# The last product of a two-layer network gets its own PSUM bank, and the last output tile leaves in two halves on two queues

## Chip, cores, metric

The kernel runs on one core of one Trainium2 chip. The metric is the device time of one execution in microseconds (us). Times inside an execution come from a profiled run and are counted from the start of its span.

## What is computed

The reference is a delta-rule attention layer followed by a feed-forward block with an exact GELU, all in float32:

```python
# q, k, v: (4 batches, 8 heads, 768 steps, 48); beta: (4, 8, 768)
k_n = k / (norm(k) + 1e-6)
for t in range(S):
    y[t]  = q[t] @ state
    state = state + beta[t] * outer(k_n[t], v[t] - k_n[t] @ state)
x = y as (batch * step, head * dim)        # 3072 x 384
h = x @ w_in                               # w_in: 384 x 2048
out = (0.5 * h * (1 + erf(h / sqrt(2)))) @ w_out   # w_out: 2048 x 384
```

## The kernel before, in words

The 768 steps are cut into NC = 12 chunks of 64 steps. A chunk has two tiles (`tiles[c, a]`, a = 0 and 1), each 128 rows of `x`: 64 steps of two batches. For each chunk the attention part makes `xT`, the transposed input of the feed-forward block. `fc1` (L668) then multiplies it by `w_in` in 16 blocks and puts the GELU of each into `G`. The second matrix product follows from `G` and `w_out_sb`.

For chunks 0 and 1 the second product is done directly (`fc2`, L680). From chunk 2 on it is a Strassen-Winograd scheme over 2 x 2 blocks: seven products of 128 x 1024 by 1024 x 192 instead of eight. `two(c, n)` (L725) issues the matmuls of product n, each product being 16 matmul instructions in the profile, all from L709 in `product`. The order in a chunk is n = 1, 5, 2, 6, 4, 7, 3. The products go to three PSUM tiles: X and Y, each with two halves of 192 columns (`X[:, 0]`, `X[:, 1]`, `Y[:, 0]`, `Y[:, 1]`), and Z. Products 6 and 7 go to `Y[:, 0]` one upon the other, and product 3, the last, goes to `Y[:, 1]`. X and Y come from the pool tag "mlp" (two buffers), which `fc1` uses too; the attention's matmuls use the tag "dn" (two buffers of two banks each).

`read2(c, n)` (L747) combines the products on VectorE after products 6, 7 and 3. After n = 6 it makes `u2` (L751). After n = 7 it makes `u3` (L754), the two halves of tile 1's output (L755, L756), sends tile 1, copies the left half of tile 0's output on ScalarE (L759), and adds Z to `u2` (L760). After n = 3 it makes the right half of tile 0's output (L762) and sends tile 0. Output tiles are 128 x 384 float32; `send` (L675) sends one as two DMAs of 64 rows (96 KB each), both issued from ScalarE's queue.

At the call level a plan gives each step a due time, and `emit` sorts the steps by it. VectorE's instructions stay in that order; the other engines' queues are ordered by the scheduler from the same list. After the last step of the plan only the last chunk's products, reads and sends are left, and then the closing of the program (L992), where the SyncE (SP) queue waits for all DMAs and the engines meet in a barrier. SP's queue otherwise carries the input loads; its last load is issued at 545.2 us.

The last chunk's c is NC - 1 = 11. Nothing but its closing steps is touched by the change.

Of the kernel before, what the change touches and what calls it, by code (L numbers as in the profile page):

```python
# [11 lines left out]
ALU = mybir.AluOpType  # L12
# [4 lines left out]
def kernel(  # L17
# [28 lines left out]
    nc = tc.nc  # L46
    B, H, S, D = q.shape
    DM, DF = moe_w_in.shape
    C = 64
    HB = 32  # L50
    NC = S // C
# [6 lines left out]
    HALF = [slice(0, C), slice(C, 2 * C)]  # L58
# [10 lines left out]
    def dn(name):  # L69
        return ps.tile([128, 2, 512], F32, tag="dn", name=name)  # L70
# [20 lines left out]
    tiles = {}  # L91
# [7 lines left out]
    for c in range(NC):  # L99
        for a in range(NA):  # L100
            u = tiles[c, a] = Unit()
# [61 lines left out]
    for p in range(2):  # L163
        nc.gpsimd.dma_start(out=bt[:, :, p, :],
                            in_=beta.rearrange("b h (c t) -> (b h) c t", t=C))
# [497 lines left out]
    DH = DM // 2  # L663
    B11, B12 = w_out_sb[:, 0:FH, 0:DH], w_out_sb[:, 0:FH, DH:]
    B21, B22 = w_out_sb[:, FH:, 0:DH], w_out_sb[:, FH:, DH:]
# [6 lines left out]
                             rhs=xTs[c][:, m, :], start=(m == 0), stop=(m == NM - 1))  # L672
        nc.scalar.activation(G[:, f, :], psH, ACT.Gelu)  # L673

    def send(u):  # L675
        for p in range(2):
            row = (2 * u.a + p) * S + u.c * C
            nc.scalar.dma_start(out=out[row:row + C, :], in_=u.o[HALF[p]])

    def fc2(u, f0, f1):  # L680
        if f0 == 0:
            u.psO = ps.tile([128, DM], F32, tag="mlp", name="psO")
        for f in range(f0, f1):
            nc.tensor.matmul(u.psO, lhsT=G[:, f, u.a * 128:(u.a + 1) * 128],  # L684
                             rhs=w_out_sb[:, f, :], start=(f == 0), stop=(f == NF - 1))
        if f1 == NF:
            u.o = wk.tile([128, DM], F32, tag="o_sb", name="o_sb")
            nc.scalar.copy(u.o, u.psO)
            send(u)
# [14 lines left out]
    A = [[G[:, k * FH:(k + 1) * FH, a * 128:(a + 1) * 128] for k in range(2)] for a in range(NA)]  # L704
    W2 = {}

    def product(ps_, lhs, rhs, first):
        for f in range(FH):
            nc.tensor.matmul(ps_, lhsT=lhs[:, f, :], rhs=rhs[:, f, :], start=first and f == 0,  # L709
                             stop=f == FH - 1, skip_group_check=not first)  # L710
# [14 lines left out]
    def two(c, n):  # L725
        if n == 1:
            W2["X"] = ps.tile([128, 2, DH], F32, tag="mlp", name="psX2")
            W2["o"] = [wk.tile([128, DM], F32, tag="o_sb", name="o_sb") for a in range(NA)]
            product(W2["X"][:, 0], A[0][0], B11, True)
        elif n == 5:  # L730
            W2["Z"] = small[0].tile([128, DH], F32, tag="z", name="psZ2")
            product(W2["Z"], W2["S"], T[1], True)
            W2["p1"] = more[0].tile([128, DH], F32, tag="p1", name="p1")
            nc.scalar.copy(W2["p1"], W2["X"][:, 0])
        elif n == 6:
            W2["Y"] = ps.tile([128, 2, DH], F32, tag="mlp", name="psY2")
            product(W2["Y"][:, 0], A[0][0], T[2], True)
        elif n == 2:
            product(W2["X"][:, 0], A[0][1], B21, False)
        elif n == 7:  # L740
            product(W2["Y"][:, 0], A[1][0], T[3], False)
        elif n == 4:
            product(W2["X"][:, 1], A[1][1], T[4], True)
        else:
            product(W2["Y"][:, 1], A[0][1], B22, True)

    def read2(c, n):  # L747
        o, X, Y, Z = W2["o"], W2["X"], W2["Y"], W2["Z"]
        if n == 6:
            W2["u2"] = more[0].tile([128, DH], F32, tag="u2", name="u2")  # L750
            nc.vector.tensor_tensor(W2["u2"], Y[:, 0], W2["p1"], op=ALU.add)  # L751
        elif n == 7:
            W2["u3"] = more[0].tile([128, DH], F32, tag="u3", name="u3")
            nc.vector.tensor_tensor(W2["u3"], Y[:, 0], W2["p1"], op=ALU.add)  # L754
            nc.vector.tensor_tensor(o[1][:, 0:DH], X[:, 1], W2["u3"], op=ALU.add)  # L755
            nc.vector.tensor_tensor(o[1][:, DH:], Z, W2["u3"], op=ALU.add)  # L756
            tiles[c, 1].o = o[1]
            send(tiles[c, 1])
            nc.scalar.copy(o[0][:, 0:DH], X[:, 0])  # L759
            nc.vector.tensor_tensor(W2["u2"], Z, W2["u2"], op=ALU.add)  # L760
        else:
            nc.vector.tensor_tensor(o[0][:, DH:], Y[:, 1], W2["u2"], op=ALU.add)  # L762
            tiles[c, 0].o = o[0]
            send(tiles[c, 0])

    def first_layer(c, f):
        fc1(c, f)
# [3 lines left out]
    def second_layer(c, n):  # L771

        two(c, n)
        if n in (1, 2):
            for h in range(2):
                mix(c, n + 1, h)
        elif n in (6, 7, 3):
            read2(c, n)
# [218 lines left out]
```

## Time and profile before

| | us |
|---|---|
| median of 5 runs | 678.8 |
| lowest and highest run | 677.83 and 679.25 |
| the profiled execution, its own time | 677.83 |
| its span, from first to last instruction | 675.8 |
| TensorE busy (share of the span) | 643.7 (95%) |
| VectorE busy | 450.7 (67%) |
| ScalarE busy | 221.0 (33%) |
| the last product's matmuls, start | 668.49 |
| last instruction on a compute engine, end | 671.76 |

The time of an execution is longer than its span by what lies before the first and after the last instruction. In the timeline a row gives start, duration, engine, line, operation, output tile, input tiles and count. In square brackets stands how long the engine was idle before it and what ended that. PE is TensorE's matmuls, PEld its weight loads, DVE VectorE, ACT ScalarE. ACTq and SPq are the queues of ScalarE and SyncE: a DMA_DIRECT2D there is the issue of a DMA, and the transfer itself comes later. A DMA's landing is when its last semaphore update is seen.

### The profile page before, as it was taken

How to read it: one execution, taken by the hardware profiler on the slowest of the kernel's cores; microseconds unless marked ns; L12 is line 12 of the kernel's file. 1: busy time of each engine (PE TensorE's matmuls, PEld its weight loads, DVE VectorE, ACT ScalarE, POOL GpSimd, SP SyncE). 2: the span in 40 equal slices, each digit the busy share in tenths (PEclk: the TensorE clock that was granted, in tenths of full speed). 3: DMA queues.
4: the chain of work that ended last, by engine and by line, in shares of the span. 5: the costliest groups of instructions: out<-in, count | busy, mean ns of one | idle time of the engine just before them, and what ended most of it. 6: DMA issues, size and time to landing. Idle time of an engine off the chain costs nothing.

```text
span 675.8 us, 21674 instructions
## 1 busy us (share of the span) xinstructions
PE 643.7 (95%) x9542; PEld 561.4 (83%) x9542; DVE 450.7 (67%) x920; ACT 221.0 (33%) x571; POOL 90.0 (13%) x91
## 2 busy tenths in 40 slices
PE   6858999998999999999999999999999999999997
PEld 5656875765689989989989989989989989989996
DVE  5999999895589856579846479846479844324021
ACT  3357754213443142242153142153142132132220
POOL 5051300302210021111021111021111010000000
PEclk9975999998999999999999999999999999999999
DMA  8875565203431233421232411211401310100101
GB/s 124 190 239 171 116 172 131 48 1 58 87 42 32 55 43 55 75 41 26 55 46 51 81 34 25 52 23 31 66 3 25 56 18 3 25 1 2 23 1 25
DMA packets 157566, 39.75 MB, mean 59 GB/s; under 512 B 149216, under 2 KB 152288, under 8 KB 157472
## 3 DMA queue, kind: packets, MB, share of 16 engines
q1 hardware_dynamic: 151424, 33.06, 25.7%
q10 hardware_dynamic: 5952, 5.12, 3.4%
q8 instruction: 75, 1.23, 0.8%
q0 software_dynamic: 96, 0.20, 0.1%
q14 instruction: 19, 0.16, 0.1%
HBM read 33.62 MB, written 4.72 MB: 57 GB/s over the span
## 4 chain that ended last, share of the span: by engine, by line
PE 75%; DVE 5%; issue 1%; POOL 0%; ACT 0%
PE psH L671 32%; PE psY L709 12%; PE psX L709 12%; PE psZ L709 4%; PE psJ L511 3%; PE psK L566 3%; PE psG L361 3%; PE psO L684 2%; PE psU L591 2%; DVE tmp L436 2%; PE psY L609 2%; DVE Nu L438 2%; PE psY L618 1%; PE psX L653 1%; DVE u L754 0%
## 5 line engine op out<-in xcount | busy, mean ns | idle before, releaser
L671 PE MATMUL psH<-xT,w_in_sb 128*128 128x256 f32 x1152 | 262.3, 384 | 2.9 <-ACT G L673 2.2
L671 PEld LDWEIGHTS psH<-xT,w_in_sb 128*128 128x128 f32 x1152 | 216.0, 191 | 34.5 <-ACT G L673 3.9
L673 ACT ACTIVATE G<-psH 128x256 f32<-128x256 f32 x192 | 73.4, 384 | 187.1 <-PE psH L671 175.1
L438 DVE TENSOR_TENSOR Nu<-Nu,tmp 128x30 f32<-128x30 f32 (+9 forms) x180 | 61.8, 343 | 6.2
L436 DVE TENSOR_TENSOR tmp<-Nu 128x30 f32<-128x30 f32 (+9 forms) x180 | 62.2, 346 | 5.1
L709 PE MATMUL psY<-w_out_sb,G 128*128 128x192 f32 x320 | 57.0, 329 | 1.1 <-DVE u L754 0.5
L709 PE MATMUL psX<-w_out_sb,G 128*128 128x192 f32 x320 | 56.2, 329 | 0.0
L709 PEld LDWEIGHTS psY<-w_out_sb,G 128*128 128x128 f32 x320 | 51.6, 190 | 2.8 <-DVE u L754 2.5
L709 PEld LDWEIGHTS psX<-w_out_sb,G 128*128 128x128 f32 x320 | 52.2, 190 | 0.7
L684 PE MATMUL psO<-w_out_sb,G 128*128 128x384 f32 x128 | 46.6, 507 | 0.2 <-DVE w_out_sb L237 0.2
L654 ACT COPY xT<-psX 128x384 f32<-128x384 f32 x24 | 11.4, 478 | 106.6 <-PE psX L653 105.5
L303 POOL TENSOR_TENSOR n<-n,half 128x16 f32<-128x16 f32 x10 | 29.5, 2950 | 89.1 <-DVE n L286 68.2
L597 ACT COPY U<-psU 64x192 f32<-64x192 f32 x96 | 30.1, 313 | 19.5 <-PE psU L591 18.3
L396 DVE TENSOR_TENSOR P<-psG,mask 128x1024 f32<-128x1024 f32 x10 | 12.2, 1221 | 35.9 <-PE psG L361 35.9
L684 PEld LDWEIGHTS psO<-w_out_sb,G 128*128 128x128 f32 x128 | 23.5, 194 | 14.1 <-DVE w_out_sb L237 0.8
L326 POOL TENSOR_TENSOR V<-V,n 128x384 f32<-128x384 f32 x22 | 21.8, 1001 | 95.1 <-DMA V<-in_v_dram 94.4
L460 POOL MEMSET Zf<- 32x512 f32 x23 | 12.4, 540 | 153.7 <-DVE Zf L451 125.2
L574 DVE TENSOR_TENSOR W<-psK,V 128x384 f32<-128x384 f32 x22 | 12.1, 552 | 30.6 <-ACT y L573 30.5
L718 DVE TENSOR_TENSOR S<-G 128x512 f32<-128x512 f32 x20 | 13.7, 687 | 25.8 <-ACT G L673 25.7
L632 DVE TENSOR_TENSOR x<-psY,y 64x192 f32<-64x192 f32 x80 | 28.2, 353 | 0.9
L709 PE MATMUL psY<-T,G 128*128 128x192 f32 x160 | 28.2, 329 | 0.0
L709 PE MATMUL psX<-T,G 128*128 128x192 f32 x160 | 28.0, 329 | 0.0
(135 smaller groups left out, 856.3 us busy)
## 6 DMA issues: line engine op xcount, KB each, us to landing
Kp<-in_k_dram SPq DMA_DIRECT2D x76, 96.0 KB, 3.4
w_out_sb<-in_moe_w_in_dram SPq DMA_DIRECT2D x24, 256.0 KB, 3.9
V<-in_v_dram SPq DMA_DIRECT2D x48, 96.0 KB, 2.9
out_dram<-o_sb ACTq DMA_DIRECT2D x48, 96.0 KB, 2.2
w_raw<-in_moe_w_out_dram SPq DMA_DIRECT2D x10, 384.0 KB, 4.0
Zf<-in_moe_w_out_dram SPq DMA_DIRECT2D x6, 384.0 KB, 4.8
Qp<-in_q_dram SPq DMA_DIRECT2D x64, 32.0 KB, 2.2
Qp<-in_q_dram SPq DMA_DIRECT2D x16, 96.0 KB, 4.2
```

The costliest lines, as they stand in the source:

```text
L303: nc.gpsimd.tensor_tensor(flat, flat, half, op=ALU.pow)
L326: engine.tensor_tensor(u.V, u.V, ns[u.c][:, u.a].unsqueeze(2).to_broadcast([128, H, D]), op=ALU.mult)
L361: nc.tensor.matmul(psG[HALF[p], r, i * NP + j, :], lhsT=u.Kt[rows, p, j, :], rhs=(u.Qt if x else u.Kt)[rows, p, j, :], start=True, stop=True)
L436: nc.vector.tensor_tensor(tmp, nu[:, j + 1:, j:j + 1].to_broadcast([128, n, j]), nu[:, j:j + 1, 0:j].to_broadcast([128, n, j]), op=ALU.mult)
L438: nc.vector.tensor_tensor(nu[:, j + 1:, 0:j], nu[:, j + 1:, 0:j], tmp, op=ALU.add)
L511: nc.tensor.matmul(psJ[to, i, :], lhsT=(xm if level else off)[rows, u, :], rhs=zf[rows, u, HB:C] if level else xm[rows, u, :], start=True, ...
L597: copy(pairs(u.U[HALF[p]], s), u.psU[HALF[p ^ s], p])
L632: nc.vector.tensor_tensor(dst, src, pairs(u.y[HALF[p ^ s]], s), op=ALU.add)
L671: nc.tensor.matmul(psH, lhsT=w_in_sb[:, f // 2, m, f % 2 * 128:(f % 2 + 1) * 128], rhs=xTs[c][:, m, :], start=(m == 0), stop=(m == NM - 1))
L673: nc.scalar.activation(G[:, f, :], psH, ACT.Gelu)
L684: nc.tensor.matmul(u.psO, lhsT=G[:, f, u.a * 128:(u.a + 1) * 128], rhs=w_out_sb[:, f, :], start=(f == 0), stop=(f == NF - 1))
L709: nc.tensor.matmul(ps_, lhsT=lhs[:, f, :], rhs=rhs[:, f, :], start=first and f == 0, stop=f == FH - 1, skip_group_check=not first)
```

## The change

For the last chunk alone:

- Product 3 is written to a PSUM tile of its own, `psV2`, from the tag "dn", instead of `Y[:, 1]`. L762 reads it there.
- Tile 0's left half (columns 0 to 191) is sent once it has been copied, by two DMAs of 64 rows from SP's queue.
- Tile 0's right half (columns 192 to 383) is sent after L762 by two DMAs of 64 rows, the upper one from SP's queue and the lower one from ScalarE's.

`send` takes the columns and the queues as arguments. The other chunks and tile 1 send as before. The program has two more DMAs than before.

```diff
-    def send(u):
+    def send(u, cols=slice(0, DM), queues=(nc.scalar, nc.scalar)):
         for p in range(2):
             row = (2 * u.a + p) * S + u.c * C
-            nc.scalar.dma_start(out=out[row:row + C, :], in_=u.o[HALF[p]])
+            queues[p].dma_start(out=out[row:row + C, cols], in_=u.o[HALF[p], cols])
...
         else:
-            product(W2["Y"][:, 1], A[0][1], B22, True)
+            W2["V"] = W2["Y"][:, 1] if c < NC - 1 else dn("psV2")[:, 0, 0:DH]
+            product(W2["V"], A[0][1], B22, True)
...
             nc.scalar.copy(o[0][:, 0:DH], X[:, 0])
             nc.vector.tensor_tensor(W2["u2"], Z, W2["u2"], op=ALU.add)
+            tiles[c, 0].o = o[0]
+            if c == NC - 1:
+                send(tiles[c, 0], slice(0, DH), (nc.sync, nc.sync))
         else:
-            nc.vector.tensor_tensor(o[0][:, DH:], Y[:, 1], W2["u2"], op=ALU.add)
-            tiles[c, 0].o = o[0]
-            send(tiles[c, 0])
+            nc.vector.tensor_tensor(o[0][:, DH:], W2["V"], W2["u2"], op=ALU.add)
+            if c == NC - 1:
+                send(tiles[c, 0], slice(DH, DM), (nc.sync, nc.scalar))
+            else:
+                send(tiles[c, 0])
```

## The prediction

> **What bounds the kernel now.** The page comes first, to see whether a saving at the very end can be hidden by anything.
>
> ```profile
> span 675.8 us, 21674 instructions
> ...
> PE 643.7 (95%) x9542; PEld 561.4 (83%) x9542; DVE 450.7 (67%) x920; ACT 221.0 (33%) x571; POOL 90.0 (13%) x91
> ...
> PE 75%; DVE 5%; issue 1%; POOL 0%; ACT 0%
> ```
>
> TensorE is busy for 95% of the span, and the chain that ended last runs over it. The change leaves TensorE's 9542 matmuls and their shapes as they are, and touches only the last chunk, so I read the timeline of the last microseconds:
>
> ```profile
> start us, us, engine line op out<-in xcount [idle before <-releaser]
> ...
> 665.28 2.76 PE L709 MATMUL psY<-w_out_sb,G 128*128 128x192 f32 x16
> 668.08 0.36 DVE L754 TENSOR_TENSOR u<-psY,p 128x192 f32<-128x192 f32 x1 [4.77 <-PE psY L709]
> 668.47 0.36 DVE L755 TENSOR_TENSOR o_sb<-psX,u 128x192 f32<-128x192 f32 x1
> 668.49 2.57 PEld L709 LDWEIGHTS psY<-w_out_sb,G 128*128 128x128 f32 x16 [0.74 <-DVE u L754]
> 668.49 2.87 PE L709 MATMUL psY<-w_out_sb,G 128*128 128x192 f32 x16 [0.45 <-DVE u L754]
> ...
> 668.90 0.32 ACT L759 COPY o_sb<-psX 128x192 f32<-128x192 f32 x1 [13.51 <-DVE o_sb L755]
> 669.01 0.35 DVE L760 TENSOR_TENSOR u<-psZ,u 128x192 f32<-128x192 f32 x1
> 669.12 3.84 ACTq L678 DMA_DIRECT2D out_dram<-o_sb  x4
> 671.40 0.36 DVE L762 TENSOR_TENSOR o_sb<-psY,u 128x192 f32<-128x192 f32 x1 [2.04 <-PE psY L709]
> ```
>
> Everything ends in one file. The seventh product (n = 7) ends at 668.04. VectorE reads it (L754), and only when that read is over (668.44) does the last product (n = 3) start, at 668.49. L762 follows, then the two DMAs of tile 0. The DMAs are in the view of line L678 over these microseconds:
>
> ```profile
> L678 ACTq DMA_DIRECT2D out_dram<-o_sb x4: 473/542/619, 669.1 to 672.3; - x4
> L678 ACTq EVENT_SEMAPHORE  x2: 17/17/17, 668.9 to 671.8; - x2
> ...
> DMA to landing us min/median/max: 2.1/2.2/2.3
> ```
>
> Durations are in ns (min/median/max). The same timeline in narrow windows puts the last two issues at 671.84 (0.47 us) and 672.34 (0.62 us): ACT's queue hands them over one after the other. The last one lands 2.3 us after its issue, at 674.6. SP's queue has been waiting for exactly this, by the view of its waits:
>
> ```profile
> SPq L992 <- DMA out_dram<-o_sb: 128.9, 2, 128.3
> ```
>
> From 674.6 to 675.8 come SP's remaining closing waits and the barrier of the engines. No compute engine works after 671.76, so whatever makes that last landing earlier shortens the span one for one.
>
> **What the Trainium skill says.** "PSUM — Partial Sum Buffer", section "PSUM bank collisions raise a hardware error", asks that accesses by two engines be ordered by bank and quadrant, not by address. The trace agrees in effect: the product into Y[:,1] waits for a read of Y[:,0]. "DMA: Bandwidth & Descriptors", section "Issuing engines are not separate DMA queues", says that issuing from two engines saves only the sequencer's issue time, since the 16 DMA engines are the same. Here that issue time is on the path. "Perfetto Trace Analysis", section "DMA Instruction — HWDGE (DVE, Sync)", says that two sequencers share one descriptor generator, locked while one uses it. The kernel's start, where SP and ACT both issue at 0.80, shows a mild form: 0.72 and 0.73 us for those two issues, against a median of 0.64 over SP's four.
>
> **The change part by part.** The program as built differs only in these tail instructions; every earlier row on every engine has the same waits.
>
> *Own bank.* For the last chunk the last product goes to psV2, and its first matmul no longer waits for VectorE. The buffer's pool, "dn", was last read by L632, long before, so nothing new is waited for. The three products before it start at 660.08, 662.68 and 665.28, 2.60 apart. So this one starts at 665.28 + 2.60 = 667.88, not 668.49 (0.61 saved), and takes 2.76 as they do, not 2.87 (0.11). It ends at 670.64 in place of 671.36: **0.72 us**, all of it on the path. L754, L755, L756 and L760 keep their times, since they depend on n = 7 (668.04); L760 ends at 669.36, before 670.64. L762 moves whole, to 670.67 to 671.03.
>
> *First half (columns 0 to 191) sent early.* Two DMAs of 48 KB on SP, released by ACT's copy L759, which ends at 669.22. At up to 0.62 each they occupy SP's queue until about 670.6, which is 0.5 us before it is needed again. Ahead of them stand input loads that were issued before 546. Their 96 KB mix with tile 1's 192 KB, which flow from about 670.2 to 671.5 now (141 GB/s over 1.4 us). At that rate 288 KB last to about 672.2, and the final data begin then (below). I cost this at nothing; the cover is the last product and DMA latency. With the cover gone it is 0.3 us at most.
>
> *Second half on two queues.* SP and ACT each send 48 KB after L762. L762's end to the first issue is 0.08 now (671.76 to 671.84), so both issue at 671.11. ACT is free: tile 1's two issues end at 670.25 now. The issue that counted was the second, at 672.34; of the 1.23 us between 672.34 and 671.11, 0.72 is the product and **0.50** is the first issue that no longer stands ahead. From issue to landing: 2.1 for an issue that starts on an empty queue, 2.3 for one behind another, both for 96 KB. Each transfer is now half, but two start together and may contend for the generator. The trace has no such pair of output transfers, so I bound it. Low: 1.8, the fastest of SP's small input transfers late in the kernel (16 and 32 KB). High: 2.3 and another 0.45. That is the delay at the start, where the other queue's data begin at 2.75 against 2.30 although both issued at 0.80; those were 512 pieces each, these are 64. I take 2.2. The landing is then at 671.11 + 2.2 = 673.3, against 674.6: **1.3 us** in all so far, of which 0.72 is the product.
>
> *Closing waits.* After its last wait ends SP goes through further semaphores of its list: five rows between 674.6 and 674.9, some 0.065 us each. In the program of before the last output DMA is on the second pair of the list. With two more DMAs, the last pair is on the third and fourth, so two rows fewer follow: **0.13 us**. From the landing to the end 1.2 becomes 1.05. SP reaches this list only after its own last issue (about 671.7), well before 673.3. The moved assignment of `o` emits nothing.
>
> *Sum.* 0.72 + 0.50 + 0.1 + 0.13 = 1.45 us. The profiled execution took 677.83 (span 675.8 and 2.0 around it), so its like would take 676.4. It was the fastest of the five runs; from the median 678.8 I get **677.4**.
>
> **The rivals.**
>
> 1. *Forecast:* gain 1.1 to 1.75 us (landing 2.55 to 1.9), 677.05 to 677.7.
> 2. *The two issues still go one after the other.* The lock or the shared engines make the later half land 2.75 after its issue. Gain 0.72 + 0.13 + 0.05 = 0.9, time 677.9. For: the 0.45 at the start. Against: there, four issues on each queue took 3.05 us in all, not the sum of both.
> 3. *The product keeps its wait*, or TensorE has another reason to stand (the change doesn't do what it says). Only the split is left, 0.7 us: 678.1. For: a gap is put down to the latest releaser, and another may stand behind it. Against: the operands of n = 3 were there by 660.97 (end of L723).
> 4. *Slower: two queues at once are dear.* At the start, with both queues issuing, landing took 4.0 to 6.2 us, median 5.1. Were the last pair to take 5.1, the end is at 671.11 + 5.1 + 1.05 = 677.3, 1.5 later: 680.3. It turns into a loss from 3.6 us. Against: those transfers were loads in 192-byte pieces with others queued behind; SP's queue is empty here, and the pieces are 768 bytes.
>
> **How the numbers follow.** A difference of 0.2% is 1.36 us, about what a measurement of this kernel can tell from no change, and the forecast lies just beyond it. Rival 1 gets 0.76 (0.62 beyond the bound, 0.14 short of it), rival 2 0.12, rival 3 0.06, rival 4 0.06 (0.05 past the bound, 0.01 short of it). So faster 0.62, same 0.33, slower 0.05. The range takes in rivals 1 to 3 (677.05 to 678.1) and about 0.4 for the median of runs that lie 1.4 us apart: 676.6 to 678.4.
>
> **What the profile after would show.** No idle before the last 16 matmuls, and their start 2.60 after those of n = 7; DVE's last row about 670.7; two issues on SP at about 669.3 and one each on SP and ACT near 671.1; the last landing near 673.3; a span near 674.3. The forecast is wrong if the last product still starts after L754's read, if SP's and ACT's last issues differ by 0.4 or more in length, if they land more than 2.6 us after issue, or if tile 1's transfers run past 672.3 and push the last pair.

## The result, and the profile after

| | before | after |
|---|---|---|
| median, us | 678.69 (47 runs) | 676.18 (26 runs) |
| lowest and highest run | 676.36 and 681.97 | 674.61 and 678.14 |
| the profiled execution, its own time | 677.83 | 674.98 |
| its span | 675.8 | 673.2 |

The ratio is 0.9969, with a 95% interval of 0.9959 to 0.9978: 2.1 us faster, from 1.5 to 2.8. The means of these runs (678.44 and 676.31) differ by 2.1 too, the medians by 2.5. The forecast was 1.45 us and a median of 677.4, within 676.6 to 678.4; the measured median lies below that range. One more run of the change, at 680.24, is on record and not among the 26; the part on the rest of the 2.1 us comes back to it.

The timeline of the last microseconds of after:

```profile
664.20 2.76 PE L709 MATMUL psY<-w_out_sb,G 128*128 128x192 f32 x16
...
666.80 2.76 PE L709 MATMUL psV<-w_out_sb,G 128*128 128x192 f32 x16
667.00 0.36 DVE L755 TENSOR_TENSOR u<-psY,p 128x192 f32<-128x192 f32 x1 [4.77 <-PE psY L709]
...
667.93 0.35 DVE L761 TENSOR_TENSOR u<-psZ,u 128x192 f32<-128x192 f32 x1
668.05 2.44 ACTq L678 DMA_DIRECT2D out_dram<-o_sb  x3
668.17 2.28 SPq L678 DMA_DIRECT2D out_dram<-o_sb  x3
669.60 0.36 DVE L766 TENSOR_TENSOR o_sb<-psV,u 128x192 f32<-128x192 f32 x1 [1.32 <-PE psV L709]
```

The last product now starts 2.60 after n = 7, before VectorE has read Y, and has no idle time ahead of it. DVE's last sum waits 1.32 for it where it waited 2.04. SP's queue appears with three issues.

The view of line L678 from 669.5 on shows the last pair, and the view of SP's waits what SP waited for (the closing, L992 before, is now L998):

```profile
L678 SPq DMA_DIRECT2D out_dram<-o_sb x1: 466/466/466, 670.0 to 670.0; - x1
L678 ACTq DMA_DIRECT2D out_dram<-o_sb x1: 498/498/498, 670.0 to 670.0; - x1
```

```profile
SPq L678 <- ACT o_sb L760: 83.9, 1, 83.9
SPq L998 <- DMA out_dram<-o_sb: 1.5, 2, 1.0
```

Both queues issue at 669.99, and the two issues hardly stretch each other: 0.47 us on SP and 0.50 on ACT (the first of the two on ACT's queue took 0.47 before). SP's 128 us of waiting at the end have become 83.9 for the left half and 1.5 for the landings.

**Where the 2.1 us are.** The two profiles differ by 2.6 us of span, but n = 7 itself starts at 664.20 in place of 665.28. The instruction stream up to there is the same, so 1.08 us are not the change's (where they come from is read further down). From n = 7's start to the end it is 10.49 before and 9.01 after, 1.48 less. I measure this stretch, "the tail", in the trace of every run below: in traces with the same closing it repeats within 0.02 us, where times scatter by over 3 us. A second number repeats too, the time of an execution less its span: its median is 2.05 before (2.00 to 2.13 in the 59 runs beside the first experiments) and 1.78 after (1.72 to 1.90 in 27 runs). So the change gives 1.48 + 0.27 = 1.75 us, and 0.35 of the 2.1 is open. The experiments take these three in turn.

### The profile page after: what moved, and what is told of

Read it like the earlier page. It is cut to its first block, busy times and chain, and to the rows that moved or that the text cites. A ratio compares the mean times of both kernels' runs of the same rounds, so it can differ in the third digit from the quotient of the medians.

```text
span 673.2 us, 21678 instructions
## 1 busy us (share of the span) xinstructions
PE 645.0 (96%) x9542; PEld 562.1 (84%) x9542; DVE 450.9 (67%) x920; ACT 220.9 (33%) x571; POOL 89.6 (13%) x91
## 4 chain that ended last, share of the span: by engine, by line
PE 76%; DVE 4%; issue 0%; POOL 0%; ACT 0%
PE psH L671 32%; PE psX L709 12%; PE psY L709 12%; PE psZ L709 4%; PE psJ L511 3%; PE psK L566 3%; PE psO L684 3%; PE psG L361 3%; PE psU L591 2%; DVE tmp L436 2%; PE psY L609 2%; DVE Nu L438 2%; PE psY L618 1%; PE psX L653 1%; PE psV L709 0%
## 5 line engine op out<-in xcount | busy, mean ns | idle before, releaser
L709 PE MATMUL psY<-w_out_sb,G 128*128 128x192 f32 x304 | 54.1, 329 | 0.6
L709 PEld LDWEIGHTS psY<-w_out_sb,G 128*128 128x128 f32 x304 | 49.1, 190 | 2.1 <-DVE u L755 1.8
L684 PE MATMUL psO<-w_out_sb,G 128*128 128x384 f32 x128 | 48.0, 519 | 0.2 <-DVE w_out_sb L237 0.2
```

## The experiments

A summary first. Counted from the first matmul of n = 7 (us), by the records of each trace:

| kernel | n = 7 at | last product starts | last issue | last landing | end (tail) | time less span (median) |
|---|---|---|---|---|---|---|
| before | 665.28 | 3.21 | 7.07 | 9.32 | 10.49 | 2.05 |
| the change | 664.20 | 2.60 | 5.79 | 7.91 | 9.01 | 1.78 |
| e1_bank | 663.96 | 2.60 | 6.35 | 8.60 | 9.76 | 2.05 |
| e2_split | 666.97 | 3.21 | 6.51 | 8.65 | 9.75 | 1.79 |
| e3_one_queue | 665.98 | 2.60 | 6.30 | 8.29 | 9.33 | 2.04 |
| g2_sp_both | 665.78 | 2.60 | 6.30 | 8.27 | 9.31 | 1.73 |
| e4_whole_rows | 666.47 | 2.60 | 5.84 | 8.27 | 9.43 | 1.77 |
| f3_list_end | 665.39 | 2.60 | 5.79 | 7.93 | 8.90 | 1.75 |
| f4_again | 669.58 | 2.60 | 5.79 | 7.92 | 9.01 | 1.77 |

By these columns the 1.48 us are 1.28 of the last issue (0.72 of the product, 0.51 of the issue that stood ahead, 0.05 between the sum's end and the first issue, which was about 0.08 and is 0.03), 0.13 of the way from issue to landing (2.25 to 2.12) and 0.07 of what follows the landing (1.17 to 1.10).

### The two parts alone

e1_bank keeps the own bank and sends as before:

```diff
-            if c == NC - 1:
-                send(tiles[c, 0], slice(0, DH), (nc.sync, nc.sync))
...
-            if c == NC - 1:
-                send(tiles[c, 0], slice(DH, DM), (nc.sync, nc.scalar))
-            else:
-                send(tiles[c, 0])
+            send(tiles[c, 0])
```

> Only the own bank of the last product; tile 0 is sent whole after L762's sum, both DMAs on ACT's queue, as before. Theory T (the tail's sum is right, and what the measured median gained beyond 1.5 us is not made by the edit): from the first matmul of n = 7 to the end of the span 10.5 us become 9.75 (0.7 less); the time 0.7 us below before, 0.9990. Rival R (the edit also shortens something outside the tail, through the bank): the span from the start to n = 7 is shorter in every run, or the time outside the span falls from 2.0 to 1.8 us here, and the time gains 1.0 us or more, 0.9985 or less.

e2_split keeps the sends and puts the last product back:

```diff
-            W2["V"] = W2["Y"][:, 1] if c < NC - 1 else dn("psV2")[:, 0, 0:DH]
+            W2["V"] = W2["Y"][:, 1]
```

> Only the sends: halves, on the queues of the change; the last product stays in Y[:, 1] and waits for the read of Y[:, 0]. Theory T: from n = 7's start to the end 10.5 becomes 9.7 to 9.8 (0.75 less: 0.5 for the second issue, 0.1 for the landing, 0.13 for the closing waits); time 0.75 us below before, 0.9989. Rival R (the split also shortens the time outside the span, since SP now ends with its own DMAs): the time less the span is 1.8 us in place of 2.0 and the time gains 1.0 us, 0.9985.

The timeline of e2_split has the old gap back:

```profile
670.19 2.87 PE L709 MATMUL psY<-w_out_sb,G 128*128 128x192 f32 x16 [0.45 <-DVE u L755]
```

The bank alone takes 0.73 off the tail, the sends alone 0.74; together 1.47, the whole 1.48. The two parts add up because they lie one behind the other on one path. (psV2 is another tile as well as another bank; which of the two the wait belonged to was not tried.) The times agree but tell less: 0.9993 (0.9982 to 1.0004) for the bank, where 0.73 us is 0.9989, and 0.9987 (0.9971 to 1.0004) for the sends, where 0.74 + 0.26 us is 0.9985. Rival R was right about the sends in its second number: with them the time less span is 1.79, with the bank alone 2.05.

### What the second queue and the halves are worth

e3_one_queue sends both pieces of the right half from ACT:

```diff
-                send(tiles[c, 0], slice(DH, DM), (nc.sync, nc.scalar))
+                send(tiles[c, 0], slice(DH, DM), (nc.scalar, nc.scalar))
```

> The change, but both DMAs of the right half on ACT's queue; the left half still early on SP's. Theory T (the issue that stands ahead is what the second queue takes away): the second issue starts 0.5 us after the first and lands 2.1 after its start; from n = 7's start to the end 9.4 us, 0.45 more than with the change. Rival (the two issues share one generator, so two queues gain nothing): the end within 0.1 of the change's 9.0.

The view of L678 around its last two issues:

```profile
L678 ACTq DMA_DIRECT2D out_dram<-o_sb x2: 473/540/607, 671.8 to 672.3; - x2
...
DMA to landing us min/median/max: 1.9/1.9/2.0
```

For the simultaneous pair of the change the same view in f4_again, where the landings are on record, has:

```profile
DMA to landing us min/median/max: 1.9/2.0/2.1
```

The second issue is 0.51 later than in the change, but the end only 0.32. Issued one behind the other, 48 KB land in 1.86 and 1.99 us, while the later one of the pair takes 2.12: that returns 0.13. Another 0.06 comes back in SP's closing list (9.33 less 8.29 is 1.04, where the change has 1.10; f3_list_end below shows why). The tail lies a little below theory T's 9.4 and well above the rival's 9.1. The times said only 0.9992 (0.9977 to 1.0006).

g2_sp_both sends both pieces from SP (`(nc.sync, nc.sync)`).

> The change with both DMAs of the right half on SP's queue, so that ACT's program has 662 instructions. Theory T for the path: as with e3_one_queue the second issue stands 0.5 us behind the first, 9.33 us from n = 7's start to the end. For the time less the span: 1.78 under both theories of the count; 2.05 would be against both.

9.31: which queue does it alone makes 0.02 us. Its ratio was 0.9974 (0.9947 to 1.0001).

e4_whole_rows keeps the two queues and drops the early left half: in e1_bank's form, the last call is `send(tiles[c, 0], queues=(nc.sync, nc.scalar))` in the last chunk.

> The change without the early left half: tile 0 goes whole (rows of 1536 bytes) after the last sum, upper rows on SP's queue, lower on ACT's. Theory T: twice the bytes in the last pair land 0.3 us later and the closing list is two rows longer (0.13): 9.4 us from n = 7's start to the end. Rival (landing is fixed latency, bytes cost nothing): 9.1 to 9.15, the closing rows alone.

```profile
DMA to landing us min/median/max: 2.2/2.3/2.4
```

That is the last pair's line in its view of L678: 96 KB each land in 2.2 and 2.4 us. The tail is 9.43, as theory T had it, in other parts: the last landing is 0.36 later (8.27 against 7.91, of which 0.03 is the later issue), and what follows it 0.06 longer (1.16 against 1.10), not 0.13. The ratio was 0.9982 (0.9970 to 0.9993).

Four kernels with the own bank make a square: whole rows on one queue have a tail of 9.76 (e1_bank), whole rows on two queues 9.43, halves on one queue 9.33, halves on two 9.01. The halves are worth 0.42 to 0.43 us with either, the second queue 0.32 to 0.33.

f3_list_end moves the last pair to the end of SP's closing list, by four smaller loads of V in the last chunk in place of two:

```diff
-            fetch_in(u.V, v, u)
+            if c == NC - 1 and a == 1:
+                for p in range(2):
+                    for r in range(2):
+                        rows = slice(c * C + r * HB, c * C + (r + 1) * HB)
+                        nc.sync.dma_start(out=u.V[p * C + r * HB:p * C + (r + 1) * HB],
+                                          in_=v[2 * a + p, :, rows, :].rearrange("h t d -> t h d"))
+            else:
+                fetch_in(u.V, v, u)
```

> The change, with the last chunk's second V tile loaded by four DMAs of 32 rows in place of two of 64 (around 508 us, off the path), so that every later DMA takes a semaphore two places on, and the last pair gets those that SP's closing list checks last. If the list's order is on the path as the prediction had it: 8.88 us from n = 7's start to the end, 0.13 less than the change, and the time 0.13 below it (not to be told by the times). If the rows are hidden behind the landing: 9.0.

The tail is 8.90, 0.11 less, with the landing 0.02 later. From the last landing to the end 1.10 becomes 0.97, by two rows: about 0.065 us for each row of the list that is left after the last landing. The rows from the last landing on are these in before and in the change:

```profile
L992 SPq EVENT_SEMAPHORE  x5: 28/28/28, 674.6 to 674.9; - x5
```

```profile
L998 SPq EVENT_SEMAPHORE  x4: 28/28/28, 672.1 to 672.3; - x4
```

So the change itself saved one row, not the two of the prediction. Its last pair stands third and fourth on the list, but ACT's half, which lands last, is the third. f3_list_end is by its tail the fastest version, and by its times (676.25, ratio 0.9965, 0.9950 to 0.9981) not to be told from the change.

### The time outside the span

In the first six kernels 2.05 us went with 665 instructions in ACT's program and 1.78 with 664. (The counts are of the program as built; the traces have 30 more rows on ACT in every kernel, 695 in before.) f1_act_row adds one to the change:

```diff
             nc.scalar.copy(W2["p1"], W2["X"][:, 0])
+            if c == NC - 1:
+                nc.scalar.copy(W2["p1"], W2["X"][:, 0])
```

> The change with one more instruction on ACT's queue: p1 is copied twice in the last chunk (L734), in ACT's 13 us of idle time. In six kernels the time less the span was 2.05 us where ACT's program has 665 instructions (before, e1_bank, e3_one_queue) and 1.77 to 1.79 where it has 664 (the change, e2_split, e4_whole_rows). Theory A (ACT's instruction count decides): 2.05 here, with 665. Theory B (it is that SP issues one of the last DMAs, which the same three do): 1.78 here. From n = 7's start to the end 9.0 us under both.

2.06, tail 9.01. f2_tile1_sp takes one from before, and leaves the closing as it was:

```diff
-            send(tiles[c, 1])
+            send(tiles[c, 1], (nc.sync, nc.scalar) if c == NC - 1 else (nc.scalar, nc.scalar))
```

> Before, with tile 1's upper rows in the last chunk sent from SP's queue: ACT has 664 instructions, and the last two DMAs are still both ACT's. Theory A: the time less the span is 1.78 us. Theory B: 2.05. From n = 7's start to the end 10.5 us under both, since the last product's wait and ACT's two last issues stand.

1.79, tail 10.50. Theory B is out, in both directions: one row on ACT's queue, off the end's path, moves 0.27 us outside the span. The ratios, 0.9977 (0.9965 to 0.9989) and 1.0001 (0.9988 to 1.0015), agree with 1.48 us alone and 0.27 us alone (0.9978 and 0.9996). I then varied the count alone, by small copies early on ACT's queue (n = 2, 8, 3, 9, 17, 33, 65):

```diff
+            for _ in range(n if c == NC - 1 else 0):
+                nc.scalar.copy(lim[:, 1:2], lim[:, 0:1])
```

> The change with two more small copies (128 x 1) on ACT's queue, in idle time early on: ACT's program has 666 instructions. Counts so far: the time less the span is 2.05 us at 665 (four kernels) and 1.78 at 664 (five). If it is odd against even counts: 1.78. If it is a limit between 664 and 665: 2.05. From n = 7's start to the end 9.0.

> The change with eight more small copies on ACT's queue: 672 instructions, a multiple of eight like 664. If even counts, or multiples of eight, are what saves the time: 1.78 us of time less span. If it is a limit between 664 and 665: 2.05. From n = 7's start to the end 9.0.

> The change with three more small copies on ACT's queue: 667 instructions. The limit between 664 and 665 fell: with 666 and 672 the time less the span was 1.82 and 1.70 us. If odd counts cost the 0.28: 2.05 here. If 665 was only a special value: 1.75 to 1.8. From n = 7's start to the end 9.0.

> The change with nine more small copies on ACT's queue: 673 instructions, 8 above 665. If what counts comes back every 8 instructions: time less span 2.05 us. If it comes back every 16 or more, or 665 is single: 1.7 to 1.8. From n = 7's start to the end 9.0.

> Seventeen more small copies: 681 instructions, 16 above 665. Period of 8 or 16: time less span 2.05 us. Period of 32 or more, or single: 1.7 to 1.8.

> Thirty-three more small copies: 697 instructions, 32 above 665. Period of 8, 16 or 32: time less span 2.05 us. Period of 64, or single: 1.7 to 1.8.

> Sixty-five more small copies: 729 instructions, 64 above 665. Any period from 8 to 64: time less span 2.05 us. Single: 1.7 to 1.8. The copies may hold up ACT's work near 120 us, so the span itself may be longer; from n = 7's start to the end 9.0.

| ACT instructions | 662 | 664 | 665 | 666 | 667 | 672 | 673 | 681 | 697 | 729 |
|---|---|---|---|---|---|---|---|---|---|---|
| time less span, us | 1.73 | 1.75 to 1.79 | 2.04 to 2.06 | 1.82 | 1.73 | 1.70 | 1.82 | 1.75 | 1.75 | 1.75 |

All seven have a tail of 9.01 to 9.02. The 1.70 is from three runs. A limit, parity, or a period of 8, 16, 32 or 64 does not explain it: 665 is the only costly count found. The rows of the whole program do not explain it either, since e3_one_queue and g2_sp_both both have 21677 and 2.04 and 1.73 us. That the 0.27 us come and go with ACT's program is shown; why 665 is dear stays open, and a part of the change's gain is therefore an accident of this kernel's count. Five of the seven had ratios of 0.9962 to 0.9982. i_act_33 and i_act_65 were slower as wholes, 1.0005 and 1.0037: their copies stand at 79 to 88 us and 77 to 98 us, between the steps by which ACT prepares the weights (L224), and these two traces lose about 2 and 4 us between 75 and 120 us.

### The rest of the 2.1 us

f4_again is the change once more.

> The change itself once more, beside before on the same chip. Theory T (1.48 us of span and 0.28 around it, the rest of the first 2.1 is where the runs fell): 1.76 us below before, 0.9974, interval reaching over 0.9969. Rival R (something else in the runs is made faster, 0.3 to 0.6 us): 0.9969 or less again, and 0.9974 at the edge of the interval or out of it. In the profile 9.0 us from n = 7's start to the end, whatever n = 7's own start.

Its ratio was 0.9984 (0.9970 to 0.9999), 1.1 us. Theory T's 0.9974 lies inside this interval and rival R's 0.9969 just outside. The two measurements, weighted by the inverse square of their half widths (0.00095 and 0.00145), give 0.9974 (0.9966 to 0.9981), where theory T's 1.75 us is 0.9974.

A stronger test of rival R takes all runs on record. A run's time less its kernel's tail and its time outside the span is what lies ahead of n = 7. That is 665.95 us in the mean of 259 runs of before, and 666.08 in 138 runs of the change (twice) and six of its variants (e1_bank, e2_split, e3_one_queue, g2_sp_both, e4_whole_rows, f1_act_row), with standard errors of 0.08 and 0.11. This takes the tail to be the same in every run of a kernel, as it is in the traces. No gain ahead of n = 7 shows, where rival R needs 0.3 to 0.6 us, so it falls: the 0.35 is where the first runs fell.

Why single measurements swing is seen in the runs of the first one. Nearly all lie in three groups, 1.3 us apart:

| group | before, us | after, us | difference of the group medians |
|---|---|---|---|
| low | 676.36 to 676.88 (8 runs) | 674.61 to 675.08 (7) | 1.65 |
| middle | 677.34 to 678.26 (13) | 675.85 to 676.35 (9) | 1.68 |
| high | 678.64 to 679.67 (24) | 677.13 to 678.14 (10) | 1.62 |

(Two runs of before, 681.69 and 681.97, and the run of the change at 680.24 are a fourth group.) Within a group the difference is 1.6 to 1.7 us. The medians differ by more because before's lies in its high group and after's in its middle one.

The windows of both profiles show where a run falls into its group. The columns are the stretch, its length, busy time and number of instructions on PE, PEld, DVE, ACT and POOL, the granted clock, DMA share and GB/s. Before:

```profile
150.00:153.00 3.00, 2.96 (x19) 1.50 (x13) 3.00 (x3) 0.00 (x0) 0.51 (x1) 1.00 0.02 5
153.00:156.00 3.00, 0.38 (x18) 0.29 (x22) 2.72 (x5) 0.98 (x2) 2.76 (x5) 1.00 0.04 7
156.00:160.00 4.00, 4.00 (x130) 2.47 (x125) 2.50 (x4) 1.15 (x2) 1.71 (x1) 0.57 0.53 99
...
165.00:640.00 475.00, 473.32 (x7144) 425.77 (x7137) 300.29 (x633) 141.98 (x351) 51.68 (x43) 1.00 0.23 39
```

After:

```profile
150.00:153.00 3.00, 3.00 (x31) 2.03 (x28) 3.00 (x3) 0.00 (x0) 0.48 (x1) 0.50 0.02 5
153.00:156.00 3.00, 3.00 (x5) 1.08 (x4) 2.75 (x5) 0.98 (x2) 2.76 (x5) 0.50 0.03 7
156.00:160.00 4.00, 3.98 (x137) 2.45 (x136) 2.17 (x4) 1.15 (x2) 1.74 (x1) 0.97 0.53 99
...
165.00:640.00 475.00, 473.32 (x7135) 426.00 (x7134) 300.11 (x633) 141.36 (x351) 51.07 (x43) 1.00 0.23 39
```

Around 153 to 156 TensorE has few matmuls to run (18 and 5). In before the half clock comes after that pause, at 156 to 160, and slows the 130 matmuls there. In after it comes ahead of the pause and in it, at 149 to 156, and is mostly over when the work comes. From 165 to 640 both are alike to the last digit (473.32). The same matmul, found in both traces by its place in the order, shows what this cost:

| the matmul that starts in before at, us | 149.0 | 152.2 | 156.0 | 160.1 | 165.1 | 640.2 |
|---|---|---|---|---|---|---|
| after starts it later (+) or earlier (-) by, us | +0.04 | +2.50 | +0.27 | -1.08 | -1.08 | -1.08 |

After loses 2.5 us at half clock where before does not, gets most of it back in the pause, and then does not lose what before loses. That is the whole 1.08 us of n = 7's start. All 18 traces agree. From the matmul at 149.0 to the one at 165.1 they take 1.1 to 1.5 us less than before where the half clock falls ahead of the pause or in it, or is missing (ten traces). They take the same within 0.1 us where it follows the pause for 3.4 us (before and four more), and 1.05 to 1.15 more where it lasts for longer after the pause (e4_whole_rows, f2_tile1_sp, f4_again). Six traces, f4_again among them, have another stretch of half clock near 68 to 76 us, and each loses 2.78 us there. These steps are about the distances between the groups: f4_again has both losses, and its own time, 680.35, is in the fourth.

The Trainium skill, "TensorE: Matmul & The Clock Gate", section "What's actually happening", says that the clock gate follows TensorE's activity in windows of 3413 ns that run free of the kernel's start. The traces agree in that their stretches at half clock, but for the last, which the end of the trace cuts off, are 3.4 us or whole multiples of it. That the clock makes the groups is read from 18 traces; no experiment moved the windows.

## Why the prediction was wrong, point by point

- **Own bank, 0.72 us: right.** The last product starts 2.60 after n = 7 and ends at 5.36; e1_bank gave 0.73. Rival 3 is out.
- **Left half early, nothing: right.** Its two SP issues (0.55 and 0.68 us) are over 0.5 us before the last one, and the packets of tile 1 and the left half end at 670.6, before those of the last pair begin at 671.1.
- **Two queues, 0.50 and 0.1 us: right,** with 0.56 and 0.13 measured. The pair's issues hardly stretched each other, so rival 2's lock did not show, and the later landing took 2.12 us where 2.2 was taken. The two terms are not one cause each: the second queue alone is worth 0.32 and the halved bytes 0.42.
- **Closing list, 0.13 us: mis-sized, 0.07.** The prediction counted two rows fewer; it was one, since ACT's half landed last and stands third on the list. f3_list_end shows that two rows are 0.13.
- **The sum for the span: right, in part by luck.** The tail is 9.01, where the working gives 9.05. The list gave 0.06 less than predicted, the last issue 0.06 more, of which 0.05 is the shorter way from the sum to the first issue.
- **"Span 675.8 and 2.0 around it": the first step that failed.** The 2.0 was carried over as a constant. It fell by 0.27 us, and f1_act_row and f2_tile1_sp show that this goes with the one row that ACT's program lost when one of its last issues went to SP. No row of the profile shows this time; only the time beside the span does. Why 665 rows cost it stays open.
- **"About 0.4 for the median of runs that lie 1.4 us apart": the second step that failed, and the larger one.** With the 0.27 the forecast would have been 677.1 and its range 676.3 to 678.1, still above the measured 676.18. The runs fall into groups 1.3 us apart, and a median jumps from group to group: before's was in the high group, after's in the middle one. Of the 1.17 us between the forecast (678.8 less 1.45) and 676.18, 0.11 is before's own median (678.69, not 678.8), 0.03 the span, 0.27 the time outside, and 0.76 this jump.
- Rival 4 is out: the pair landed after 1.86 and 2.12 us, not 5.1.

## What to carry to other kernels

At the end of a kernel, list what follows the last matmul one by one (sum, issue, second issue, landing, closing waits): nothing there was hidden in these runs, parts added up, and such a sum came out here to 0.05 us, two errors of 0.06 cancelling. Ask of the last result only what must be last: its own bank, half of the bytes, one issue per queue. A change of 0.2% is to be measured on a stretch that starts at the same instruction in both traces, and on the time outside the span, since single times of this kernel scatter by over 3 us while that stretch repeats within 0.02. A forecast of a median needs the groups into which the runs fall, and five runs did not show them.

## What the runs showed of the hardware that was not expected

- The time of an execution less its span was 2.04 to 2.06 us with 665 instructions in ACT's program and 1.70 to 1.82 with nine other counts.
- SP and ACT issuing at the same moment took 0.47 and 0.50 us for 64 rows of 768 bytes each, against 0.47 for each alone (g2_sp_both, e3_one_queue), although the same two queues took 0.72 and 0.73 at the kernel's start for 512 pieces of 192 bytes each. In f4_again SP's 48 KB landed 1.86 us after the common issue and ACT's 2.12; one behind the other they took 1.86 and 1.99.
- Two 96 KB stores issued together landed after 2.2 and 2.4 us, two of 48 KB after 1.86 and 2.12: halving the bytes saved some 0.3 us.
- Each row of SP's closing list after the last landing cost about 0.065 us.
- A half-clock stretch of 3.4 us or its multiple went with a loss of 2.78 us near 68 to 76 us, and around 149 to 165 us with one between nothing and 2.6 us, by whether it fell in a pause of TensorE (18 traces).
